# Moving PSUM evictions and one batch's normalisation from ScalarE to VectorE in a fused attention and gated-MLP kernel, with new instruction orders

## The chip, the core and the metric

The kernel runs on one core of a Trainium2 chip. Five engines work on their own instruction streams and meet only at semaphores: TensorE (PE in the profile, its weight loads PEld), VectorE (DVE), ScalarE (ACT), GpSimd (POOL) and SyncE (SP), which here issues every DMA. TensorE writes its results into PSUM; VectorE and ScalarE read them from there. The metric is the device time of one execution in microseconds (us). Three runs of the kernel before gave 223.18 us as the median, 222.97 the lowest and 224.26 the highest.

## What is computed

The inputs are q, k, v of 4 batches x 8 heads x 768 positions x 64 elements, and the weights of a gated MLP. Attention lets each query see only 6 chunks of 32 keys, chosen by an upper bound on the chunk's scores; the MLP mixes positions with a 768 x 768 matrix. Cut to what matters:

```python
ub = sum(max(q * k_min[chunk], q * k_max[chunk]))        # per query and chunk of 32 keys, causal
sel = the 6 chunks with the largest ub
attn = softmax(where(sel & causal, q @ k.T / 8, -1e9))
x = (attn @ v), heads side by side                       # 4 x 768 x 512
h = gelu_tanh(x @ w_in)                                  # 512 -> 1024
u, vg = h[..., :512], h[..., 512:]
v_n = (vg - mean(vg)) / sqrt(var(vg) + 1e-6) * g_ln
v_s = w_sg @ v_n + b_sg                                  # over the 768 positions
out = x + (u * v_s) @ w_out
```

## The kernel before

The unit of the attention is a pair of heads, 16 of them, numbered 0 to 15; four pairs make a batch, numbered 0 to 3 (the fourth to be done is batch 3). For each pair the kernel does the following; the names in brackets are the tags of the operations in the code, and they are used in all that follows.

- Rows of q and k are loaded by DMA (qn, kn), v too (vn). TensorE transposes them into PSUM (qtr, ktr, two halves each, line 508). The transposed q is copied out of PSUM (qev, line 561) and the transposed k too (kev, line 539; pairs 4 to 7 need two copies for each half, one for each head). VectorE reduces each chunk of k to its minimum and maximum (kmm, line 532). POOL makes a clipped q (rel, line 565), casts q (qcast, line 572), and casts v (vcast, line 577).
- The chunk bounds come from TensorE (ub, lines 602 and 649, for one pair or for two at once); VectorE transposes them (utr), finds the sixth largest (m8), compares (dn) and transposes back (dt). SP copies the resulting mask rows into place (qd) for pairs from 4 on.
- Scores (sc, lines 717, 757, 763) go to PSUM, ScalarE takes their exponential (exp, lines 723 and 772), POOL zeroes the part above the diagonal (aff, lines 728 and 779), TensorE multiplies by v (pv, and pvd for the diagonal blocks, which waits for aff; lines 795 and 802), VectorE divides by the row sum (rcp, xs; lines 810 and 812).

After the fourth pair of a batch its x is transposed (xtr, line 829; batch 2 by DMA) and copied out of PSUM as x^T (xev, line 832). Then the MLP of the batch runs, interleaved with the attention of later pairs: six products for the gate half (hv, line 844) with a GELU on ScalarE (gv, 848), mean and variance on VectorE (bns, bna, var), the inverse root on POOL (rstd, line 859, one instruction for the batch), the normalisation vhat (six instructions, line 874 on ScalarE or line 879 on VectorE), eight products for the other half (hu, line 890) with a GELU (gu, 895), eight products with w_sg (pt, line 907), a scale and a product on VectorE (vs, gt), six products with w_out (ou, line 926), the sum with x (os) and the store (st). The transposes of w_sg (wst) are copied out by VectorE (wev). The casts of w_in (wic) are POOL's, and hv of the first batch needs all four.

Two switches say which engine copies out of PSUM: a pair in KDVE or QDVE has its kev or qev on VectorE, otherwise on ScalarE; VH and XEV say for each batch which engine does vhat and xev. `evac` (line 423) emits the one instruction or the other. Where vhat is on ScalarE, POOL has two small instructions more (nmr, nmr2, lines 862 and 865). PSUM has two buffers for scores (PSC) and four for the rest (PSG); transposes mostly use two of these four, so a late eviction holds back the next transpose.

Nothing is ordered at run time. `_build` numbers the operations in the order in which it makes them; `TABLE` holds for each engine, SP's DMA queue included, the order in which it runs them, the PSUM buffer of each tile, and where TensorE gets extra idle matmuls that write nothing that is used (15 in all). `place` and `link` turn this into semaphore waits. An engine works strictly in its order, so an operation that waits holds everything behind it on its engine.

Of the kernel before, what the change touches and what calls it, by code (L numbers as in the profile page):

```python
# [260 lines left out]
def _build(nc, ctx, q, k, v, w_in, g_ln, w_sg, b_sg, w_out, out):  # L261
# [3 lines left out]
    F = DFF // 2  # L265
# [23 lines left out]
    def T(name, shape, dt):  # L289
        return ctx.enter_context(nc.sbuf_tensor(name, list(shape), dt))  # L290
# [25 lines left out]
    VH = ("act","dve","dve","dve")  # L316
# [10 lines left out]
    KDVE = (2,)  # L327
    QDVE = (2, 3)
    WEV = "dve"
    XEV = ("act",)*4  # L330
# [29 lines left out]
    vhat = [T(f"vhat{i}", [128, NT, F], BF16) for i in range(2)]  # L360
# [474 lines left out]
    def moe_h(b):  # L835
# [31 lines left out]
        for qt in range(NT):  # L867
# [5 lines left out]
            elif VH[b] == "act":  # L873
                P.op("act", lambda e, qt=qt: e.activation(vhat[s][:, qt, :], vg[qt], ACTF.Identity,  # L874
                                                          bias=nmr[s][:, qt:qt + 1], scale=rstd[s][:, qt:qt + 1]),
                     (F / 1.2 + 85, F / 1.2 + 185), ("vhat", b, qt),
# [107 lines left out]
    for p in range(4, NP + 4):  # L984
# [38 lines left out]
    "act": (  # L1023
# [11 lines left out]
    "dve": (  # L1035
# [34 lines left out]
        "2310011001113201111000110023011000001123101101222333233223233233322232222310110032101011032001101032"  # L1070
        "11000113200123010310311323203212101302"),
    "filler": (
        "43:9 54:1 59:3 77:2"),
}


# [57 lines left out]
```

## Time and profile before

| what | us |
|---|---|
| median of three runs | 223.18 |
| the profiled execution, its own time | 222.71 |
| its span, first to last instruction | 221.0 |
| TensorE busy | 204.0 |
| VectorE busy | 173.1 |
| ScalarE busy | 165.1 |
| GpSimd busy | 101.6 |

The profile is of one execution. Its page gives busy times, the chain of work that ended last, and groups of instructions; other views give the busy time of each engine in chosen stretches of the span, the instructions in order of time with the idle time ahead of them, and sums of waits by who waited for whom. In a row of a group, the number behind the bar is the busy time, then the mean length of one instruction in ns, then the idle time ahead of them. In a row of waits, the numbers are the sum in us, how often, and the longest.

### The profile page before, as it was taken

What the parts mean: (1) busy time and instruction counts of PE and PEld (TensorE: products, weight loads), DVE (VectorE), ACT (ScalarE), POOL (GpSimd) and SP (SyncE); (2) the same over time, 40 slices, a digit from 0 to 9 for tenths busy, and PEclk for the clock granted to TensorE, in tenths of its full rate; (3) what the DMA queues carried; (4) which work ended last, traced back from release to release, by engine and by line L of the source; (5) the groups of instructions that cost most, each with busy time, mean ns of one, the idle gap of its engine ahead of it and who ended that gap; (6) DMA issues with size and microseconds to landing.
All of it is one profiled execution on the core that took longest, in us unless ns stands there. A gap on an engine that the chain in (4) does not pass through costs nothing.

```text
span 221.0 us, 5927 instructions
## 1 busy us (share of the span) xinstructions
PE 204.0 (92%) x2332; PEld 133.8 (61%) x2348; DVE 173.1 (78%) x500; ACT 165.1 (75%) x249; POOL 101.6 (46%) x153
## 2 busy tenths in 40 slices
PE   7778999879979999988999999999799999999992
PEld 3356767745646667677556676777445669545641
DVE  3499684649949898885799998987698767688993
ACT  3857899987999696989868977899867898753000
POOL 6363975985416939745170057998402114001000
PEclk9999999999999999999999999999999999999998
DMA  7999999899077997895969977959502002001316
GB/s 152 220 241 237 230 227 334 180 243 310 14 201 202 214 205 216 197 200 127 200 135 215 188 185 164 266 133 154 155 6 77 20 0 98 0 3 74 116 55 230
DMA packets 87451, 35.47 MB, mean 160 GB/s; under 512 B 80129, under 2 KB 82433, under 8 KB 87425
## 3 DMA queue, kind: packets, MB, share of 16 engines
q1 hardware_dynamic: 87424, 35.11, 68.2%
q8 instruction: 18, 0.29, 0.6%
q14 instruction: 9, 0.07, 0.1%
HBM read 24.77 MB, written 6.29 MB: 141 GB/s over the span
## 4 chain that ended last, share of the span: by engine, by line
PE 60%; ACT 12%; DVE 10%; DMA 8%; POOL 4%; issue 2%; SPq 2%; DVEq 0%; POOLq 0%
PE PSG L907 14%; PE PSG L926 8%; PE PSC L717 7%; PE PSG L508 6%; PE PSG L844 6%; PE PSG L890 6%; DMA vn<-in_v_dram 6%; ACT E L772 4%; PE PSG L795 4%; PE PSG L649 3%; ACT vhat L874 2%; DVE W L532 2%; DMA qn<-in_q_dram 2%; ACT KA L425 2%; SPq L492 2%
## 5 line engine op out<-in xcount | busy, mean ns | idle before, releaser
L723 ACT ACTIVATE E<-PSC 128x1024 bf16<-128x1024 f32 (+1 forms) x72 | 63.4, 919 | 8.6 <-PE PSC L717 8.2
L532 DVE TENSOR_REDUCE W<-PSG 128x12 f32<-128x384 f32 x64 | 32.7, 544 | 9.8 <-PE PSG L508 9.6
L728 POOL TENSOR_SCALAR_AFFINE_SELECT E<-E 128x768 bf16<-128x768 bf16 x24 | 20.5, 863 | 41.2 <-ACT E L723 41.0
L717 PE MATMUL PSC<-QA,KA 128*128 128x128 bf16 (+2 forms) x336 | 37.2, 246 | 0.0
L907 PE MATMUL PSG<-wsgT,vhat 128*128 128x384 bf16 x192 | 35.0, 326 | 0.7 <-ACT vhat L874 0.5
L717 PEld LDWEIGHTS PSC<-QA,KA 128*128 128x128 bf16 x336 | 24.2, 98 | 8.6 <-ACT E L723 2.2
L895 ACT ACTIVATE uT<-PSG 128x384 bf16<-128x384 f32 x32 | 15.3, 489 | 16.0 <-PE PSG L890 15.7
L907 PEld LDWEIGHTS PSG<-wsgT,vhat 128*128 128x128 bf16 x192 | 17.9, 98 | 12.0 <-ACT vhat L874 0.8
L890 PE MATMUL PSG<-xT,winb 128*128 128x384 bf16 x128 | 24.1, 327 | 0.8 <-ACT uT L895 0.8
L572 POOL CAST QA<-qT 64x768 bf16<-64x768 f32 (+1 forms) x28 | 23.3, 836 | 2.8 <-ACT qT L425 1.6
L772 ACT ACTIVATE E<-PSC 128x1024 bf16<-128x1024 f32 (+1 forms) x24 | 20.8, 920 | 4.6 <-PE PSC L763 4.4
L913 DVE SCALAR_TENSOR_TENSOR PSG<-PSG,glnT,bsgbc 128x384 f32<-128x384 f32 x32 | 19.8, 621 | 5.6 <-PE PSG L907 5.2
L844 PE MATMUL PSG<-winb,xT 128*128 128x512 bf16 x91 | 21.6, 379 | 1.1 <-ACT qT L425 0.5
L926 PE MATMUL PSG<-woutb,uT 128*128 128x512 bf16 x86 | 21.6, 379 | 0.5
L795 PE MATMUL PSG<-vx,E 128*128 128x65 bf16 x480 | 19.9, 194 | 1.2 <-POOL vx L577 0.8
L425 ACT ACTIVATE KA<-PSG 128x384 bf16<-128x384 f32 (+1 forms) x38 | 18.4, 492 | 1.9 <-PE PSC L717 1.2
L795 PEld LDWEIGHTS PSG<-vx,E 128*128 128x128 bf16 x480 | 17.4, 98 | 3.6 <-POOL vx L577 1.1
L933 DVE TENSOR_TENSOR osb<-PSG,XS 128x512 f32<-128x512 f32 x24 | 16.2, 684 | 4.0 <-PE PSG L926 3.5
L853 DVE BATCH_NORM_STATS2 stats<-vgb 128x6 f32<-128x512 f32 x24 | 15.9, 684 | 4.0 <-ACT vgb L848 3.7
L917 DVE TENSOR_TENSOR uT<-PSG,uT 128x384 bf16<-128x384 f32 x32 | 17.6, 555 | 0.8
L848 ACT ACTIVATE vgb<-PSG 128x512 f32<-128x512 f32 x24 | 14.0, 597 | 5.4 <-PE PSG L844 4.6
L812 DVE TENSOR_TENSOR XS<-PSG,rden 128x384 bf16<-128x384 f32 x32 | 17.4, 552 | 0.7
(87 smaller groups left out, 337.1 us busy)
## 6 DMA issues: line engine op xcount, KB each, us to landing
kn<-in_k_dram SPq DMA_DIRECT2D x32, 192.0 KB, 4.5
qn<-in_q_dram SPq DMA_DIRECT2D x32, 192.0 KB, 4.4
vn<-in_v_dram SPq DMA_DIRECT2D x16, 384.0 KB, 5.1
out_dram<-osb SPq DMA_DIRECT2D x24, 256.0 KB, 2.4
uT<-in_moe_w_sg_dram SPq DMA_DIRECT2D x4, 384.0 KB, 5.0
KA<-INDF SPq DMA_DIRECT2D x16, 96.0 KB, 3.7
vgb<-in_moe_w_in_dram SPq DMA_DIRECT2D x3, 512.0 KB, 8.0
QA<-Dt SPq DMA_DIRECT2D x24, 36.0 KB, 2.4
```

Source lines behind the costliest of these rows:

```text
L425: P.op("act", lambda e: e.activation(dst(), src(), ACTF.Copy), act(n), tag, reads=reads, writes=writes, ps=ps, shift=shift)
L532: P.op("dve", lambda d, m=m, op=op, src=src, h0=h0, h1=h1: d.tensor_reduce(W[w][:, m, 12 * h0:12 * h1].rearrange("p (h c) -> p h c", h=h1 ...
L572: P.op("pool", lambda g, i=i, r0=r0, r1=r1: g.tensor_copy(QA[w][i or 0][r0:r1, :], qT[r][r0:r1, :]), gps(S, 250 if i == 1 else 150), ("qca ...
L717: r = e.matmul(t.ap()[:, o:o + n], KA[w][i][:, 128 * kb:128 * kb + 128], QA[w][i][:, q0:q0 + n], start=True, stop=True)
L723: P.op("act", lambda e, t=t, c0=c0, c1=c1, i=i: e.activation(E[es][:, i, c0:c1], t.ap()[:, 0:c1 - c0], ACTF.Exp, scale=SCALE), act(c1 - c0 ...
L728: P.op("pool", lambda g, ev=ev: g.affine_select(ev, ev, pattern=[[0, NT], [1, 128]], compare_op=ALU.is_ge, fill=0.0, base=0, channel_multi ...
L772: P.op("act", lambda e, t=t, c0=c0, c1=c1, n=n: e.activation(E[es][:, :, c0:c1], t.ap().rearrange("p (i x) -> p i x", i=2)[:, :, 0:n], ACT ...
L795: r = e.matmul(t.ap()[:, 65 * qb:65 * qb + 65], E[es][:, i, a:a + 128], vx[w][:, kb, i, :], start=first, stop=False, skip_group_check=True)
L844: r = e.matmul(t.ap()[:, 0:F], xT[s][:, dk, 128 * qt:128 * qt + 128], winb[:, dk, F:DFF], start=(dk == 0), stop=(dk == NDK - 1))
L890: r = e.matmul(t.ap()[:, 0:TG], winb[:, dk, 128 * fb:128 * fb + 128], xT[s][:, dk, TG * tg:TG * tg + TG], start=(dk == 0), stop=(dk == NDK ...
L907: r = e.matmul(t.ap()[:, 0:TG], vhat[s][:, sb, 128 * fb:128 * fb + 128], wsgT[:, sb, TG * tg:TG * tg + TG], start=(sb == 0), stop=(sb == N ...
L926: r = e.matmul(t.ap()[:, 0:DM], gT[s][:, fb, 128 * qt:128 * qt + 128], woutb[:, fb, :], start=(fb == 0), stop=(fb == NF - 1))
```

## The change

Four settings move work from ScalarE to VectorE, and every order in `TABLE` is replaced by another.

```diff
-    VH = ("act","dve","dve","dve")
+    VH = ("dve","dve","dve","dve")
...
-    KDVE = (2,)
-    QDVE = (2, 3)
+    KDVE = (2, 5)
+    QDVE = (2, 3, 4, 5)
     WEV = "dve"
-    XEV = ("act",)*4
+    XEV = ("dve","dve","act","dve")
...
-                     (F / 1.2 + 85, F / 1.2 + 185), ("vhat", b, qt),
+                     (705, 812), ("vhat", b, qt),
...
     "filler": (
-        "43:9 54:1 59:3 77:2"),
+        "54:9 43:1 81:2"),
```

In instructions: six vhat of batch 0, twelve xev of batches 0, 1 and 3 (batch 2 has none, it is transposed by DMA), four kev of pair 5 (two halves, two heads) and four qev of pairs 4 and 5 become VectorE's; nmr and nmr2 of batch 0 are gone from POOL. The cost pair of line 876 is read by nothing that runs. The extra idle matmuls go from 15 to 12.

The orders are lists of numbers (from 444 on, the same operation has a number two lower after the change). Read back into tags, these are the places of the new orders that the prediction speaks of; the old order stands first in each pair.

```
SP at the start    before: kn_0 kn_0 qn_0 qn_0 kn_2 qn_1 qn_1 kn_2 kn_1 kn_1 ...
                   after:  qn_0 qn_0 kn_0 kn_0 kn_1 kn_1 qn_1 qn_1 kn_2 kn_2 ...
VectorE, first     before: kmm_0 x4, utr_0 m8_0 dn_0, kmm_2 kev_2, dt_0, kmm_1 x4 ...
                   after:  kmm_0 x4, kmm_1 x4, utr_0 m8_0 dn_0 dt_0 ...
ScalarE, batch 0   before: ... exp_3_2 kev_5 kev_5 exp_3_3 qev_4 xev xev qev_4 xev qev_5 qev_5 gv_0_1 kev_5 kev_5 gv_0_0 ...
                   after:  ... exp_3_2 exp_3_5 gv_0_1 gv_0_0 gv_0_5 ...
VectorE, batch 0   after:  ... xs_2_1 qev_4 kev_5 kev_5 kmm_5 kmm_5 rcp_3_0 xev xs_3_0 rcp_3_1 xs_3_1 qev_5 xev qev_5 bns_0_1 ...
                           ... bna_0_4 dn_4 var_0 kmm_7 dt_4 kmm_7 vhat vhat wev_4 vhat vhat vhat wev_5 vhat kmm_6 kmm_6 vs_0_1_3 ...
POOL, batch 1      before: ... wsub_10 aff_8_1 vcast_8 qcast_10 rstd_1 aff_8_0 rel_13 vcast_9 wsub_13 rel_12 ...
                   after:  ... aff_8_1 wsub_10 wsub_11 rel_12 vcast_10 vcast_9 rstd_1 qcast_12 vcast_8 ...
POOL, pairs 11-13  before: ... aff_11_0 qcast_15 vcast_13 aff_12_0 vcast_15 vcast_14 wsub_14 aff_12_1 wsub_15 aff_13_1 ...
                   after:  ... aff_11_0 qcast_14 aff_11_1 qcast_14 qcast_13 rel_15 wsub_14 aff_12_0 qcast_15 aff_12_1 wsub_15 aff_13_1 ...
SP, v rows         before: ... vn_5 vn_4 ... qd_7_0 vn_7 st_0_0 qd_7_1 kn_10 qn_11 qn_11 vn_6 kcp_8 ...
                   after:  ... vn_4 ... st_0_2 vn_6 ... qd_6_1 st_0_1 qd_6_0 vn_5 ... st_0_5 kn_10 vn_7 ...
```

More of the change, by code (lines that the diff above doesn't have):

```diff
@@ L1006 @@
     "pe": (
[16 rows of a table removed]
-    "act": (
[11 rows of a table removed]
-    "dve": (
[16 rows of a table removed]
-    "pool": (
[14 rows of a table removed]
[16 rows of a table added]
+    "act": (
[9 rows of a table added]
+    "dve": (
[17 rows of a table added]
+    "pool": (
[14 rows of a table added]
     "slots": (
-        "1032203030210120010003201301110123012001010002312130100001102310101010110320101100333232223323232332"
-        "3223233223000110230110011010033101010101110032001001000112301111012332323233232222332323332232001101"
-        "2310011001113201111000110023011000001123101101222333233223233233322232222310110032101011032001101032"
-        "11000113200123010310311323203212101302"),
+        "0201213133101220001003102211100023010011000112331022110101102301000100101321110101333232323322232332"
+        "2223233323100111230000010010022111110101110032110101001103200111012332322233232322332223332332010101"
+        "2300000100102311111011100023011000011123011101222333233223233233322232223310110023101011032001101032"
+        "11000113202011300113121012230230013132"),
     "filler": (
-        "43:9 54:1 59:3 77:2"),
+        "54:9 43:1 81:2"),
 }
```

111 rows, old and new, of the table TABLE are left out of this document.

## The prediction, made before the changed kernel was run

> **What bounds the kernel now.** First the page's list of busy times (the span is 221.0), then the view that gives busy time by stretch, cut at the places where the work changes: the start, the attention of batch 0 (to the first hv), its MLP up to the first pt, then the rest.
>
> ```profile
> PE 204.0 (92%) x2332; PEld 133.8 (61%) x2348; DVE 173.1 (78%) x500; ACT 165.1 (75%) x249; POOL 101.6 (46%) x153
> ```
> ```profile
> core 0: us, PE busy (x) PEld busy (x) DVE busy (x) ACT busy (x) POOL busy (x), PEclk, DMA share, GB/s
> 0.00:13.40 13.40, 10.20 (x60) 5.20 (x61) 7.04 (x25) 7.09 (x12) 6.71 (x21) 1.00 1.09 191
> 13.40:46.60 33.20, 29.53 (x551) 21.95 (x553) 24.03 (x82) 28.93 (x42) 23.47 (x34) 1.00 1.03 243
> 46.60:65.10 18.50, 16.57 (x138) 9.53 (x140) 14.09 (x50) 16.41 (x31) 9.48 (x14) 1.00 0.68 181
> 65.10:95.40 30.30, 30.10 (x349) 21.09 (x353) 26.17 (x79) 25.09 (x38) 21.15 (x32) 1.00 0.92 209
> 95.40:107.20 11.80, 10.06 (x157) 8.02 (x155) 8.02 (x25) 10.81 (x16) 4.83 (x6) 1.00 0.76 156
> 107.20:145.00 37.80, 37.57 (x390) 25.14 (x395) 35.70 (x108) 30.41 (x48) 18.13 (x25) 1.00 0.88 195
> 145.00:158.40 13.40, 11.81 (x224) 9.34 (x224) 9.04 (x22) 12.18 (x18) 10.18 (x16) 1.00 0.73 144
> 158.40:190.00 31.60, 31.28 (x330) 19.86 (x331) 25.34 (x72) 25.92 (x36) 6.28 (x7) 1.00 0.13 44
> 190.00:221.00 31.00, 26.93 (x141) 13.62 (x142) 23.68 (x47) 8.28 (x15) 1.33 (x1) 0.98 0.23 85
> ```
>
> TensorE is the bound: 204.0 of 221.0. Its 17 us of idle time are all that any reordering can win, and they lie in few places. Length less busy time gives 3.20 us at the start, 3.67 in the attention of batch 0 (call it stage A), 1.93 in its MLP (stage B), 0.20 from 65.1 to 95.4, 1.74 up to 107.2 (stage C), 0.23 up to 145, 1.59 up to 158.4 (stage D), 0.32, and 4.07 at the end. The start waits for rows of q and k and the end for the last products and stores; the change touches neither in substance, since what stands first in the new orders still has to wait for the q and k of pair 0. So the question is what becomes of the 8.9 us in A to D. In A and B ScalarE is the busiest of the other engines, 28.93 of 33.20 and 16.41 of 18.50; in C 10.81 of 11.80.
>
> **The price of a moved instruction.** These are the groups by form: the four that leave ScalarE, and the nearest forms on VectorE. The single row behind them, from the instructions in order of time, shows six vhat on VectorE in one run.
>
> ```profile
> L874 ACT ACTIVATE vhat<-vgb,nmr,rstd 128x512 bf16<-128x512 f32 x6 | 4.6, 811 | 0.0
> ...
> L425 ACT ACTIVATE xT<-PSG 128x768 bf16<-128x768 bf16 x12 | 9.6, 809 | 1.6 <-PE PSG L829 1.6
> ...
> L425 ACT ACTIVATE KA<-PSG 64x384 bf16<-64x384 f32 x16 | 7.7, 483 | 0.4 <-DVE W L532 0.2
> ...
> L425 ACT ACTIVATE qT<-PSG 128x384 f32<-128x384 f32 x28 | 13.5, 489 | 4.4 <-PE PSG L508 3.8 <-POOL QA L572 0.4
> ...
> L428 DVE COPY wsgT<-PSG 128x768 bf16<-128x768 bf16 x6 | 3.3, 544 | 2.0 <-PE PSG L477 1.9
> ...
> L428 DVE COPY qT<-PSG 128x384 f32<-128x384 f32 x4 | 2.2, 550 | 0.2 <-PE PSG L508 0.2
> ...
> L879 DVE TENSOR_SCALAR vhat<-vgb,mv,rstd 128x512 bf16<-128x512 f32 x18 | 8.5, 542 | 0.9 <-POOL rstd L859 0.8
> ```
> ```profile
> 115.55 2.84 DVE L879 TENSOR_SCALAR vhat<-vgb,mv,rstd 128x512 bf16<-128x512 f32 x6
> ```
>
> ScalarE loses 4.6 for vhat, 9.6 for the twelve xev, 1.9 for four of the 16 half-height kev (7.7 / 4) and 1.9 for four of the 28 qev (13.5 / 7): 18.0 us, so 147 of 221 are left. On VectorE an instruction takes less of the queue than its length, because the next one begins before it ends: six vhat in 2.84 us is 0.47 each at a length of 542 ns, and so is 8.5 / 18. I take 0.47 for a vhat, and for the copies their rows less the same 0.07: 0.48 for a qev (row 550) and a kev, 0.48 to 0.54 and here 0.50 for an xev (the wsgT copy has its shape, type and source: 544). VectorE gains 6 x 0.47 + 12 x 0.50 + 8 x 0.48 = 12.7 us and stands at 185.8. An xev gets 0.27 us shorter in itself, a qev 0.06 longer.
>
> The Trainium skill, "VectorE: DVE Perf Modes", section "The DRAIN you can't avoid", says that the next VectorE instruction does not start until the pipe of the one before is empty. By that rule the 26 instructions would cost their full length, about 14.2 us, and VectorE's room in stage A, worked out below, would be 2.6 instead of 3.4 us. The row above speaks against it for instructions without a wait between them.
>
> **Stage A, 13.4 to 46.6.** Twelve of the moved instructions lie here or just behind: 4 kev, 4 qev, 4 xev. The end of the stage on ScalarE, in order of time:
>
> ```profile
> 38.38 0.81 ACT L425 ACTIVATE xT<-PSG 128x768 bf16<-128x768 bf16 x1
> ...
> 40.34 0.98 ACT L425 ACTIVATE KA<-PSG 64x384 bf16<-64x384 f32 x2
> ...
> 41.23 1.01 ACT L772 ACTIVATE E<-PSC 128x1024 bf16<-128x1024 f32 x1
> ...
> 46.01 0.87 ACT L425 ACTIVATE qT<-PSG 128x384 f32<-128x384 f32 x2
> ...
> 46.90 1.28 ACT L848 ACT_TABLE_LOAD   x1
> ```
> ```profile
> 44.77 0.50 PE L829 MATMUL PSG<-identB,XS 128*128 128x128 bf16 x6 [0.67 <-ACT qT L425]
> ...
> 46.78 0.81 PE L844 MATMUL PSG<-winb,xT 128*128 128x512 bf16 x3 [0.52 <-ACT qT L425]
> ```
>
> The row at 41.23 is the last exponential of pair 3, on which pv, xs, xtr, xev and so the first hv depend; ahead of it stand one xev and two kev that go, 0.81 + 0.98 = 1.8 us. Behind it TensorE waits twice for a qev (0.67 and 0.52), and the table for the GELU is loaded at 46.90 only because two qev stand ahead of it; with no copy between the last exponential and the first gv that load falls into ScalarE's idle time. That is the gain side. The other side is VectorE: 24.03 us busy and 12 x 0.48 to 0.50 = 5.8 more make 29.8 of 33.2, so the stage can shorten by at most 3.4 us, and only if VectorE never waits, where it now idles 9.2. Ends of the range: 0 and -3.4 (below nothing is the second rival). I take -1.5, near the 1.8 that leaves the queue in front of the last exponential, and less than that because VectorE has its share of idling. Rows of w_in are not behind this: the casts on POOL stand ahead of hv in both orders, and 23.47 of 33.20 leaves POOL room.
>
> **Stage B, 46.6 to 65.1.** The six vhat took ScalarE 4.6 us between gv, gu and two kev, and pt waits for the last of them. In the new order they follow rstd directly with two wev between: 6 x 0.47 + 2 x 0.50 = 3.8 us. ScalarE falls from 16.41 by 4.6, by 1.0 for two kev and by 1.3 for the load to 9.5; VectorE rises from 14.09 by 2.8, less one kmm (0.5) that goes behind vs, to 16.4. So VectorE allows 2.1, TensorE's idle time 1.93. Ends 0 and -1.9; I take -1.2. nmr and nmr2 on POOL are worth nothing, they ran beside rstd. Against it: ub_4 needs rel_5, which needs qev_5, now VectorE's very last instruction ahead of the MLP; the first hv covers 0.81 us of a copy and a rel (0.67, below). I add 0.3, between 0 and 0.6.
>
> **Stage C, 95.4 to 107.2.** Two waits of TensorE that the orders and the move touch:
>
> ```profile
> 96.93 0.63 PE L795 MATMUL PSG<-vx,E 128*128 128x65 bf16 x15 [0.80 <-POOL vx L577]
> ...
> 102.61 0.50 PE L829 MATMUL PSG<-identB,XS 128*128 128x128 bf16 x6 [0.33 <-ACT qT L425]
> ```
>
> The first is pv_6: the issue of v of pair 6 stands eleven places earlier on SP now. The other is ScalarE's queue, which loses four xev, 9.6 / 3 = 3.2 us. VectorE takes 2.0 and stands at 10.0 of 11.8: room for 1.8, TensorE's idle time 1.74. Ends 0 and -1.7; I take -1.0. On the other side v of pair 5 goes behind two qd_6 on SP, which wait for dt_6, and two os and a vs go ahead of dt_6 on VectorE:
>
> ```profile
> 79.64 0.78 DVE L677 STREAM_TRANSPOSE Dt<-Dn 128x576 bf16<-128x576 bf16 x1
> ...
> 80.34 0.65 DVE L933 TENSOR_TENSOR osb<-PSG,XS 128x512 f32<-128x512 f32 x1
> ```
> ```profile
> 90.34 0.62 PE L795 MATMUL PSG<-vx,E 128*128 128x65 bf16 x15
> ```
> ```profile
> vn<-in_v_dram SPq DMA_DIRECT2D x16, 384.0 KB, 5.1
> ```
>
> On the clock of before: dt_6 ends at 80.42 + 3 x 0.65 = 82.4, the issue some 2 later, 5.1 to land and 0.8 for the cast (1.61 for two, row below) make 90.3, and pv_5 began at 90.34. What is won ahead of it shifts both. I take 0; ends 0 and 1.3, two more instructions of that kind ahead of dt_6.
>
> **Stage D, 145 to 158.4.** Here nothing moves from ScalarE; the order of POOL changes.
>
> ```profile
> 150.23 0.35 PE L802 MATMUL PSG<-vx,E 128*128 128x65 bf16 x6 [0.50 <-POOL E L728]
> ...
> 153.41 1.61 POOL L577 CAST vx<-vn 128x768 bf16<-128x768 f32 x2 [0.88 <-DMA vn<-in_v_dram]
> ...
> 155.18 0.86 POOL L728 TENSOR_SCALAR_AFFINE_SELECT E<-E 128x768 bf16<-128x768 bf16 x1
> ...
> 156.10 0.54 PE L802 MATMUL PSG<-vx,E 128*128 128x65 bf16 x12 [1.09 <-POOL E L728]
> ```
>
> aff_12_1 (155.18) stood behind two casts of v that waited 0.88 us for their DMA; TensorE waited 1.09 for it, and 0.50 for aff_11_0. In the new order both casts come after aff_13_0. The 1.59 cannot all be had: ScalarE is busy 12.18 of 13.40, which leaves 1.2. I take -1.0, ends 0 and -1.2.
>
> **What else the new orders cost.** In batch 1 rstd now stands behind rel_12 and two vcast on POOL:
>
> ```profile
> L565 POOL TENSOR_SCALAR rT<-qT 128x576 f32<-128x576 f32 x16 | 10.7, 666 | 4.4 <-ACT qT L425 3.3 <-DVE qT L428 1.0
> ```
> ```profile
> 112.19 0.49 ACT L425 ACTIVATE qT<-PSG 128x384 f32<-128x384 f32 x1
> ...
> 114.07 1.34 POOL L859 TENSOR_TENSOR rstd<-rstd,neghalf 128x6 f32<-128x6 f32 x1
> ...
> 118.76 1.14 PE L907 MATMUL PSG<-wsgT,vhat 128*128 128x384 bf16 x6
> ```
>
> rel_12 needs the qev that ends at 112.68; 0.67 for it and 1.61 for two casts (the row at 153.41) give 115.0, where rstd began at 114.07. That is 0.9 later, and vhat ended at 115.55 + 2.84 = 118.4, 0.4 ahead of pt: +0.5 on the path, ends 0 and 1.4 (no slack). The long stretch to 145 has nothing to give (TensorE 37.57 of 37.80, VectorE 35.70); for order effects there and in the two other full stretches I add 0.2, from -0.3 to 1.0.
>
> **Sum.** -1.5 - 1.2 - 1.0 - 1.0 + 0.3 + 0.5 + 0.2 = -3.7. The profiled execution took 222.71 us, its span and 1.7 around it, so 219.0; the median of the runs is 0.47 above that execution, so 219.5 for a median.
>
> **The rivals.** *VectorE takes the place of ScalarE, no change.* If VectorE keeps 3.4 of its 9.2 us of idle time in A, 2.1 of 4.4 in B and 1.8 of 3.8 in C, the stages stay as long as they are; D gives 1.0, the new waits take 1.0, and the time is 223.2. For it: those idle times are waits for TensorE's results, which a fuller queue does not remove, and every transpose into the two shared PSUM buffers now waits for VectorE's turn. Against it: 29.8, 16.4 and 10.0 us still fit, and VectorE already runs at 35.70 of 37.80 elsewhere.
>
> *Slower: VectorE's idle time stays.* The same mechanism past its break-even, which is 37% of the idle time kept in A and 48% in B and C. With two thirds kept, A is 24.03 + 5.8 + 6.1 = 35.9 (+2.7), B 14.09 + 2.3 + 2.9 = 19.3 (+0.8), C 8.02 + 2.0 + 2.5 = 12.5 (+0.7); with D and the new waits cancelling that is 222.71 + 4.2, for a median 227.4.
>
> *All of it.* Each stage at its end, -3.4 - 1.9 - 1.7 - 1.2 = -8.2, and no new wait: 215.0.
>
> **How the numbers follow.** The forecast, gains of 2 to 5.5 us and so 217.7 to 221.5, gets 0.53; no change 0.22; slower 0.18; all of it 0.07. One per cent is 2.2 us, about what a measurement of this kernel can tell from no change. Faster takes the forecast without the 0.06 of it above 221, and the last case: 0.54. Same takes 0.22 + 0.06 = 0.28, slower 0.18. The range from 216.2 to 225.4 leaves out about 0.05 below and 0.15 above; the likeliest case's own is 217.7 to 221.5.
>
> **What would show it.** Right, if the first hv starts near 45.1 instead of 46.78, the table load ahead of it is done before hv ends, the first pt comes about 17.6 us after the first hv instead of 18.5, the 0.80 before pv_6 and the 1.09 before the diagonal blocks of pair 12 are gone, and VectorE is busy about 90% up to the first pt. Wrong, if TensorE's idle time in A and B is as long as before with VectorE named as what ended it, if rstd of batch 1 leaves a gap over 1.4 us ahead of pt, or if casts of v are waited for at pv_5.

## The result, and the profile after

The changed kernel takes 216.95 us (median of 4 runs, 215.63 to 218.14); the kernel before takes 223.59 (median of 4). The ratio is 0.970, 95% interval 0.963 to 0.977: 3% faster, where 3.7 us, 1.7%, was forecast. The profiled execution took 216.26 with a span of 214.5, 6.5 less than the 221.0 before. In the experiment with rstd first, two of the six executions, the profiled one (221.57) among them, were slow, so its time below is that of the other four, and its rows are read for what waits on what and not for how long.

Beside the orders, the new `TABLE` gives 110 of the 332 PSUM tiles another buffer. The runs below that keep the old orders keep the old buffers too, and those with the new orders have the new ones (experiment 8, which exchanges the lists of POOL and SP alone, has the new ones).

The busy times of the changed kernel, from its page:

```profile
PE 202.6 (94%) x2331; PEld 134.4 (63%) x2345; DVE 183.1 (85%) x526; ACT 149.9 (70%) x223; POOL 101.3 (47%) x151
```

VectorE gained 10.0 us with 26 instructions and ScalarE lost 15.2. TensorE's idle time fell from 17.0 to 11.9, which is 5.1 of the 6.5 us; the other 1.4 are busy time (204.0 before, 202.6 now), spread over many lines. The prediction had counted on idle time alone. The view by stretch, changed kernel, cut at the same events as the one of before (the columns are PE, PEld, DVE, ACT, POOL):

```profile
13.40:45.00 31.60, 29.19 (x554) 21.72 (x554) 28.57 (x94) 24.35 (x32) 24.55 (x36) 1.00 1.15 260
45.00:62.10 17.10, 16.41 (x141) 9.88 (x144) 15.29 (x52) 11.13 (x22) 8.55 (x11) 1.00 0.73 174
...
91.50:102.50 11.00, 10.91 (x167) 8.84 (x168) 10.07 (x35) 9.58 (x14) 8.41 (x11) 1.00 0.84 207
...
140.70:152.30 11.60, 11.52 (x221) 9.20 (x218) 9.22 (x22) 11.28 (x17) 9.02 (x13) 1.00 0.64 118
```

Length less the first number is TensorE's idle time: 2.41 in A (3.67 before), 0.69 in B (1.93), 0.09 in C (1.74), 0.08 in D (1.59). In B, C and D nearly all of it went. TensorE's rows of the changed kernel at the ends of the stages, in order of time:

```profile
40.68 0.63 PE L795 MATMUL PSG<-vx,E 128*128 128x65 bf16 x15 [0.70 <-ACT E L772]
...
43.78 0.51 PE L829 MATMUL PSG<-identB,XS 128*128 128x128 bf16 x6 [0.61 <-DVE XS L812]
...
45.17 0.81 PE L844 MATMUL PSG<-winb,xT 128*128 128x512 bf16 x3 [0.54 <-DVE xT L428]
46.16 0.72 PE L649 MATMUL PSG<-qT,W 64*32 64x288 f32 x16 [0.18 <-POOL rT L565]
...
62.24 1.14 PE L907 MATMUL PSG<-wsgT,vhat 128*128 128x384 bf16 x6
...
91.94 0.62 PE L795 MATMUL PSG<-vx,E 128*128 128x65 bf16 x15
...
93.02 0.62 PE L795 MATMUL PSG<-vx,E 128*128 128x65 bf16 x15
...
117.17 0.55 PE L508 MATMUL PSG<-identF,kn 128*128 128x128 f32 x3 [0.52 <-DMA kn<-in_k_dram]
...
150.20 0.35 PE L802 MATMUL PSG<-vx,E 128*128 128x65 bf16 x6
```

The first hv starts at 45.17, the first pt 17.07 later and without a wait. The products with v of pair 6 (91.94 and 93.02, one row for each head) and the diagonal products of pair 12 (150.20) have no bracket any more: those waits are gone. What is left in A is named by ScalarE once and by VectorE twice. ScalarE at the same place, changed kernel:

```profile
39.33 1.30 ACT L772 ACTIVATE E<-PSC 128x1024 bf16<-128x1024 f32 x2 [0.40 <-PE PSC L763]
40.65 1.28 ACT L848 ACT_TABLE_LOAD   x1
```

The table load follows the last exponential directly and has ended 3.2 us before the first hv.

The next table says where each kernel stands at five events, as starts of TensorE's work in us with the weight load included (so up to 0.23 ahead of the matmul's row). "Old" and "new" are the orders of before and of the changed kernel. The column for pair 6 is the start of the same products in all rows, those of its head 1: in the old orders they are the first of pair 6's two heads, in the new ones they follow head 0.

| kernel | first hv | first pt | pv of pair 6, head 1 | last hv, batch 1 | first hv, batch 2 | span |
|---|---|---|---|---|---|---|
| before | 46.55 | 65.12 | 96.92 | 109.93 | 158.38 | 221.0 |
| changed | 44.94 | 62.13 | 92.99 | 105.03 | 152.31 | 214.5 |
| moves in old orders | 48.50 | 69.53 | 102.56 | 115.39 | 163.60 | 226.2 |
| new orders, no moves | 47.56 | 67.67 | 99.04 | 113.36 | 160.34 | 222.7 |
| vhat back | 44.97 | 64.74 | 96.11 | 108.15 | 154.81 | 217.0 |
| copies back | 48.08 | 65.59 | 96.27 | 110.60 | 157.83 | 220.2 |
| POOL's order in D only | 46.87 | 65.45 | 97.39 | 110.39 | 157.82 | 220.4 |
| v of pair 6 early | 46.98 | 65.55 | 97.63 | 110.84 | 158.85 | 221.5 |
| old POOL and SP orders | 55.86 | 73.08 | 108.63 | 120.60 | 176.16 | 238.4 |
| four copies doubled | 47.15 | 64.77 | 96.37 | 108.42 | 155.55 | 217.8 |
| four copies back | 44.53 | 61.68 | 93.68 | 106.02 | 152.85 | 215.1 |

From row two less row one: A gives 1.61, B 1.38, the stretch to pair 6 0.94, C's rest 0.97, from there to batch 2 1.17, the end 0.43. Each row is one execution, and a few tenths are scatter: kernels with the same orders up to the first hv have it at 46.55, 46.87 and 46.98 (before, POOL's order in D only, v of pair 6 early) and at 44.94, 44.87 and 44.39 (changed, and experiments 6 and 9). Most of that lies ahead of the first scores, which start at 13.49 before and at 13.96 in the changed kernel. From the first scores to the first hv it is 33.06 before and 30.98 in the changed kernel, 2.1 less.

### The profile page after: what moved, and what is told of

Its sections match the earlier page's. It is cut to its first block, busy times and chain, and to the rows that moved or that the text cites. A ratio compares the mean times of both kernels' runs of the same rounds, so it can differ in the third digit from the quotient of the medians.

```text
span 214.5 us, 5915 instructions
## 1 busy us (share of the span) xinstructions
PE 202.6 (94%) x2331; PEld 134.4 (63%) x2345; DVE 183.1 (85%) x526; ACT 149.9 (70%) x223; POOL 101.3 (47%) x151
## 4 chain that ended last, share of the span: by engine, by line
PE 72%; DVE 11%; ACT 7%; DMA 4%; issue 2%; SPq 1%; POOL 1%; DVEq 0%
PE PSG L907 13%; PE PSC L717 12%; PE PSG L926 9%; PE PSG L844 7%; PE PSG L508 7%; PE PSG L795 6%; PE PSG L890 5%; DVE W L532 3%; ACT E L772 3%; PE PSG L649 3%; PE PSG L802 2%; DMA kn<-in_k_dram 2%; PE PSC L367 2%; PE PSG L829 2%; PE PSC L757 2%; ACT KA L425 2%
## 5 line engine op out<-in xcount | busy, mean ns | idle before, releaser
L848 ACT ACTIVATE vgb<-PSG 128x512 f32<-128x512 f32 x24 | 14.2, 597 | 13.9 <-PE PSG L844 13.0
L565 POOL TENSOR_SCALAR rT<-qT 128x576 f32<-128x576 f32 x16 | 10.9, 683 | 15.7 <-ACT qT L425 11.0
```

## The experiments

The two theories at the outset: the gain comes from relieving ScalarE (theory 1), or from the orders, whichever engine copies (theory 2).

### 1. The moves alone, in the old orders

```diff
 (settings VH, KDVE, QDVE, XEV as in the changed kernel; all orders as before, but:)
-ScalarE:  ... each xev, kev_5, qev_4, qev_5 of the 20 at its place
+VectorE:  ... the same instructions, at the time at which ScalarE had run them
-ScalarE:  vhat_0 x6 between gv, gu and kev
+VectorE:  ... dn_4 dt_4 wev_3 vhat_0 x6 kmm_7 kmm_7 wev_4 ...
```

> The old orders with all 26 instructions moved to VectorE, each put into VectorE's old order at the time it had on ScalarE (the six vhat behind wev_3); nothing else is reordered. Theory 1, relieving ScalarE is what wins in batch 0 and ahead of batch 1: 220 to 221.5, the first hv 1 to 2 us earlier, the first pt 2 to 3 us earlier, the wait of 1.09 ahead of the diagonal blocks of pair 12 still there. Theory 2, the new orders win and the engine of a copy matters little: 223 to 224, or 1 to 3 us slower because VectorE's order was not made for it.

227.21 us (226.76 to 227.94), ratio 1.018 (1.011 to 1.024): slower than before. The two waits of TensorE just ahead of the first hv, its longest one of B, VectorE ahead of that, and the view of B, all of this kernel:

```profile
46.41 0.51 PE L829 MATMUL PSG<-identB,XS 128*128 128x128 bf16 x6 [1.34 <-DVE qT L428]
...
48.73 0.81 PE L844 MATMUL PSG<-winb,xT 128*128 128x512 bf16 x3 [0.82 <-DVE qT L428]
...
67.32 0.49 PE L477 MATMUL PSG<-identB,wsb 128*128 128x128 bf16 x6 [2.84 <-DVE wsgT L428]
```
```profile
62.46 3.31 DVE L879 TENSOR_SCALAR vhat<-vgb,mv,rstd 128x512 bf16<-128x512 f32 x6
65.70 1.01 DVE L532 TENSOR_REDUCE W<-PSG 128x12 f32<-128x384 f32 x2
66.63 0.54 DVE L428 COPY wsgT<-PSG 128x768 bf16<-128x768 bf16 x1
```
```profile
48.50:69.50 21.00, 16.93 (x137) 10.32 (x140) 19.20 (x58) 11.23 (x22) 9.15 (x12) 0.97 0.68 177
```

The two waits before hv that ScalarE's qev had caused (0.67 and 0.52) are now VectorE's, and longer. Six vhat in one run and two kmm stand in front of a wsgT copy that frees the buffer of the next transpose, and TensorE stops for 2.84. VectorE had room by its busy time (19.20 of 21.00); the copies stood at the wrong places. The granted clock of the stage is 0.97: from 68.05 to 71.47, right behind the long wait, it is 0.50. TensorE is busy for 206.5 us in this kernel and for 204.0 before, so a part of the 4.4 us lost is slower work and not waiting. Theory 1 falls.

### 2. The new orders without the moves

```diff
 (orders as changed, but the 26 moved instructions on ScalarE again, each at the time at which VectorE had run it; nmr, nmr2 on POOL again; settings as before)
```

> The new orders with all 26 instructions back on ScalarE, each at the time it had on VectorE; POOL has nmr and nmr2 of batch 0 again. Theory 1: 219.5 to 221.5, the first hv and the first pt about where they were before, pair 12 without its wait. Theory 2: 216.5 to 218.

224.47 us (224.07 to 225.93), ratio 1.007 (1.004 to 1.011). TensorE in this kernel:

```profile
43.43 0.63 PE L795 MATMUL PSG<-vx,E 128*128 128x65 bf16 x15 [1.68 <-ACT E L772]
...
66.83 0.88 PE L508 MATMUL PSG<-identF,kn 128*128 128x128 f32 x6 [1.68 <-ACT KA L425]
```

Theory 2 falls too. Against before (223.59 and 222.85 in the two sessions), the moves alone cost 4.4 and the orders alone 1.6, and both together gain 6.6. Theory 3, formed here: every eviction needs a place in a strict queue, and moves and orders only win as a pair. What the two runs do not show is that the copies have to be on VectorE: they stand at times taken from the other engine's order, and no run looked for the best places on ScalarE for all 26 (experiment 11 does it for four).

### 3 and 4. One half of the moves back

```diff
 vhat back:   the six vhat of batch 0 on ScalarE at VectorE's times, nmr and nmr2 on POOL; the rest as changed
 copies back: xev, kev_5, qev_4, qev_5 on ScalarE at VectorE's times; vhat stays on VectorE
```

> The new kernel with only the six vhat of batch 0 back on ScalarE. Theory 1: the first pt about 1.4 us later after the first hv, 218 to 219, and nothing else changes. Theory 2: 216.5 to 217.5.

> The new kernel with the twelve xev, four kev and four qev back on ScalarE, vhat left on VectorE. Theory 1: the first hv about 1.5 us later, stage C about 1 us longer, 219 to 220. Theory 2: 216.5 to 217.5.

Vhat back: 219.00 us (218.73 to 222.01), ratio 0.984 (0.975 to 0.993). Copies back: 222.05 us (221.51 to 222.96), ratio 0.995 (0.992 to 0.999). By the medians the vhat are worth 2.0 us and the copies 5.1, together 7.1, where taking both back costs 7.5: within the new orders the two halves add up, as far as intervals of one to two us can tell. By the table the vhat work in B alone (the first hv is where it was, the first pt 2.61 later); the copies cost 3.14 up to the first hv and 2.29 between pair 6 and the last hv of batch 1. The kernel with vhat back, TensorE and ScalarE:

```profile
63.90 0.88 PE L508 MATMUL PSG<-identF,kn 128*128 128x128 f32 x6 [1.68 <-ACT KA L425]
```
```profile
62.17 0.48 ACT L895 ACTIVATE uT<-PSG 128x384 bf16<-128x384 f32 x1
62.54 0.81 ACT L874 ACTIVATE vhat<-vgb,nmr,rstd 128x512 bf16<-128x512 f32 x1
63.36 0.48 ACT L425 ACTIVATE KA<-PSG 64x384 bf16<-64x384 f32 x1
```

A copy of k of pair 7 (63.36) stands behind a vhat and a GELU, with one more vhat ahead of these, and the transpose of k of pair 6, which needs the buffer that it frees, waits 1.68. The kernel with the copies back, ScalarE around the last exponentials of pair 3:

```profile
39.49 0.82 ACT L425 ACTIVATE xT<-PSG 128x768 bf16<-128x768 bf16 x1
40.18 1.04 ACT L772 ACTIVATE E<-PSC 128x1024 bf16<-128x1024 f32 x1
...
42.00 0.48 ACT L425 ACTIVATE KA<-PSG 64x384 bf16<-64x384 f32 x1 [0.41 <-DVE W L532]
42.39 0.36 ACT L772 ACTIVATE E<-PSC 128x256 bf16<-128x256 f32 x1
```

The last exponential starts at 42.39; in the changed kernel both are done at 40.63. A copy ahead of it has itself to wait for a kmm (0.41). This is the step of stage A as forecast. It is not all of the 3.14 us, as the view of this kernel up to its first hv shows:

```profile
13.40:48.10 34.70, 30.65 (x552) 22.76 (x552) 23.45 (x82) 29.00 (x42) 24.60 (x36) 0.95 1.11 256
```

TensorE is busy for 30.65 us, where the changed kernel has 29.19 for as much work: from 43.03 to 46.45 its granted clock is 0.50. So 1.5 of the 3.1 us are slower work, and the waits gave the other half. The slow stretch begins right behind TensorE's wait of 1.68 for the last exponential, which ended at 42.81. The kernel without the moves has a wait of the same length (43.43, experiment 2) and its profiled execution no such stretch there, so when a wait has this price stays open.

### 5. POOL's order in stage D alone

```diff
 (before, POOL only)
-... aff_10_0 qcast_15 rel_15 qcast_14 aff_11_0 ... vcast_15 vcast_14 wsub_14 aff_12_1 wsub_15 aff_13_1 ...
+... aff_10_0 aff_11_0 qcast_15 rel_15 qcast_14 ... wsub_14 aff_12_1 wsub_15 aff_13_1 vcast_15 vcast_14 ...
```

> The kernel before, with POOL's order changed at one place only: the two casts of v of pairs 15 and 14 go behind the last diagonal mask of pair 13, and the first diagonal mask of pair 11 moves up right behind the one of pair 10. No instruction leaves ScalarE. Theory 1 (stage D is bound by the masks' place on POOL, and nothing else of the change is needed there): the waits of 0.50 and 1.09 us ahead of the diagonal products of pairs 11 and 12 are gone, from the scores of pair 12 to the second hv of batch 2 it takes about 9.4 us instead of 11.0, everything ahead of it stays, and the time is 1.0 to 1.6 us less, a ratio near 0.994. Rival (ScalarE is the limit of stage D, or the casts of v behind the masks make a wait of their own): the waits move to another engine and the time is within 0.3 us of before.

222.03 us (220.41 to 222.72) against 223.06 for the kernel before in the same session, ratio 0.995 (0.992 to 0.998). The same stretch, from the last products with w_out of batch 1 to the first hv of batch 2 (the expectation's "second hv"), in this kernel, in the one before and in the changed one:

```profile
145.80:157.80 12.00, 11.60 (x221) 9.16 (x220) 8.63 (x21) 11.42 (x17) 8.30 (x12) 1.00 0.63 143
```
```profile
145.30:158.40 13.10, 11.51 (x222) 9.13 (x221) 8.74 (x21) 11.88 (x18) 10.01 (x15) 1.00 0.72 140
```
```profile
141.00:152.30 11.30, 11.22 (x219) 9.07 (x217) 8.92 (x21) 10.98 (x16) 8.72 (x13) 1.00 0.65 118
```

POOL's places alone give 1.1 of the 1.8 that this stretch became shorter, with both waits gone, and theory 1's number for D holds. The rest goes with the new orders of the other engines: TensorE has 0.4 less to do in the stretch and 0.3 less idle time, and ScalarE, at 97% of it, has 16 instructions there, against 18 before.

### 6. rstd of batch 1 first

```diff
 (changed, POOL only)
-... wsub_10 wsub_11 rel_12 vcast_10 vcast_9 rstd_1 ...
+... wsub_10 wsub_11 rstd_1 rel_12 vcast_10 vcast_9 ...
```

> The changed kernel, with one step of POOL's order put back: rstd of batch 1 goes ahead of the relative-position add of pair 12 and of the casts of v of pairs 10 and 9. Theory (my step for it, +0.5 us, was a real cost): rstd starts about 1 to 2 us earlier, the idle time of TensorE ahead of the first pt of batch 1 goes, and the time is 0.4 to 0.8 us less. Rival: the late rstd lies beside other work of TensorE, or the two casts of v and the rel behind it become late for pair 9, 10 and 12 instead, and the time is the same within 0.3 us or longer.

218.4 us (217.71 to 218.91), ratio 0.978 (0.974 to 0.983): not faster than the changed kernel; the median is 1.5 us above it, with intervals that overlap. The theory falls: that step was no cost to be had back. This kernel's POOL, VectorE, SP and TensorE:

```profile
110.40 1.34 POOL L859 TENSOR_TENSOR rstd<-rstd,neghalf 128x6 f32<-128x6 f32 x1 [1.97 <-DVE rstd L857]
...
112.35 1.80 POOL L577 CAST vx<-vn 128x768 bf16<-128x768 f32 x2
```
```profile
112.89 3.37 DVE L879 TENSOR_SCALAR vhat<-vgb,mv,rstd 128x512 bf16<-128x512 f32 x6
```
```profile
113.21 0.37 SPq L500 DMA_DIRECT2D vn<-in_v_dram  x1
```
```profile
116.40 2.11 PE L907 MATMUL PSG<-wsgT,vhat 128*128 128x384 bf16 x12 [0.39 <-DVE vhat L879]
120.84 0.55 PE L508 MATMUL PSG<-identF,kn 128*128 128x128 f32 x3 [2.33 <-DMA kn<-in_k_dram]
```

Two things happen. The vhat start at 112.89, 1.15 after rstd's end, because VectorE's own list has transposes and maxima first (at 112.23 it still runs maxima for 0.74); rstd did not hold them. And the casts of v, now behind rstd, free their buffer later: the issue of v of pair 13 waits at the head of SP's list until 113.21, with k of pair 12 four places behind it, and TensorE waits for that k, 2.33 us in this execution. In the changed kernel the cast comes first, SP goes on at 109.34, and rstd ends just in time:

```profile
108.60 0.74 DVE L857 TENSOR_SCALAR rstd<-mv 128x6 f32<-128x6 f32 x1
...
111.58 2.81 DVE L879 TENSOR_SCALAR vhat<-vgb,mv,rstd 128x512 bf16<-128x512 f32 x6
```
```profile
108.48 1.61 POOL L577 CAST vx<-vn 128x768 bf16<-128x768 f32 x2
110.06 1.34 POOL L859 TENSOR_TENSOR rstd<-rstd,neghalf 128x6 f32<-128x6 f32 x1
```

### 7. v of pair 6 early

```diff
 (before, SP only)
-... st_0_2 st_0_1 qd_6 qd_7 vn_7 st_0_0 qd_7 kn_10 qn_11 qn_11 vn_6 ...
+... st_0_2 vn_6 st_0_1 qd_6 qd_7 vn_7 st_0_0 qd_7 kn_10 qn_11 qn_11 ...
```

> The kernel before, with one transfer issued earlier: v of pair 6 goes nine places forward on SP, right behind the store of t of pair 0 of that stage's list, so that the 0.80 us that TensorE waited in front of the products with v of pair 6 should go. Theory 1 (that wait was on the path): the products of pair 6 start 0.8 us earlier and the time is 0.4 to 0.8 us less. Rival (ScalarE's queue sets the end of stage C, so the wait only moves to the transposes behind it): the products start earlier, the first hv of batch 1 does not, and the time is the same within 0.3 us.

222.66 us (221.21 to 223.18) against 223.06, ratio 0.997 (0.994 to 1.000). The wait of 0.80 ahead of pair 6 is gone, and the profiled execution has another of 1.13 earlier:

```profile
89.07 0.61 PE L795 MATMUL PSG<-vx,E 128*128 128x65 bf16 x15 [1.13 <-ACT E L723]
```

The edit made this wait itself. In the kernel's order these products need the PSUM buffer that VectorE frees with a sum with x (os_0_4), and that sum needs its output tile back from the store st_0_1, which the edit put behind v of pair 6 on SP. This kernel's VectorE:

```profile
88.23 0.69 DVE L933 TENSOR_TENSOR osb<-PSG,XS 128x512 f32<-128x512 f32 x1 [1.75 <-DMA out_dram<-osb]
```

The sum waits 1.75 us for the store and ends at 88.92, 0.15 ahead of the products. So the run does not tell what the early v is worth by itself. At most 0.6% came of it, perhaps nothing: undecided.

### 8. The old orders of POOL and SP

```diff
 (changed; POOL and SP in the orders of before)
```

> The changed kernel with the orders of POOL and SP of the kernel before; the orders of TensorE, VectorE and ScalarE and the moved instructions stay as changed. Theory 3 (the placing of the copies on TensorE, VectorE and ScalarE is what moves and orders win together; POOL and SP matter in stages C and D alone): the first hv and the first pt come within 0.5 us of the changed kernel's, the 0.8 us ahead of pair 6 and the 1.6 us of stage D are lost again, and the time is 2 to 3 us longer, near 219.5. Rival (the orders of all engines must fit each other from the start): waits on POOL and on loads show up in the first 60 us, the first pt is 2 us or more later, and the time is at 222 or above.

240.11 us (239.35 to 240.69), ratio 1.075 (1.070 to 1.080). My expectation of 219.5 was wrong by 20 us, and the rival is right. Sums of TensorE's waits in this kernel (us in all, times, longest):

```profile
PE PSG L795 <- POOL vx L577: 3.6, 2, 2.1
PE PSG L802 <- POOL E L728: 2.0, 1, 2.0
PE PSG L602 <- POOL W L551: 2.0, 1, 2.0
PE PSC L717 <- DMA KA<-INDF: 1.5, 1, 1.5
```

The first hv is already 10.9 us late. POOL is nowhere near full (101 us of 238), and yet the two old orders, under new ones for the other engines, cost more than everything else tried here; which of the two costs how much was not separated. TensorE is busy for 209.6 us here and for 202.6 in the changed kernel, at a granted clock of 0.979 and 0.999 in the mean, so up to 7 of the 23 us are slower work behind the waits.

### 9 to 12. Is the changed kernel at its end?

```diff
 kn_12 early (changed, SP):    - ... kn_12 qn_14 ... vn_13 kcp_10 qd_8 kn_13 kn_12 ...
                               + ... kn_12 kn_12 qn_14 ... vn_13 kcp_10 qd_8 kn_13 ...
 four copies doubled (changed, in evac, VectorE's branch, pair 5's kev only):
+    e.tensor_copy(an idle tile, src())
     e.tensor_copy(dst(), src())
 four copies back (changed, kev_5 on ScalarE):
-... exp_3 exp_3 exp_3 exp_3_5 gv_0_1 ...
+... kev_5 kev_5 exp_3 exp_3 exp_3 exp_3_5 kev_5 kev_5 gv_0_1 ...
 both: four copies back and kn_12 early
```

> The changed kernel, with one transfer issued earlier: the second half of k of pair 12 goes nine places forward on SP, right behind the first half, ahead of v of pair 13, whose issue waits until its buffer is cast. Theory (in the changed kernel TensorE waits 0.52 us in front of the first transpose of k of pair 12 because this load stands behind v of pair 13, and with rstd put first 2.33 us for the same reason): that wait is gone and the time is 0.3 to 0.6 us less than the changed kernel's 216.95, a ratio to the kernel before near 0.968. Rival (the transposes of pair 12 have slack behind them, or the load pushes others back): the wait goes and shows up within the next 20 us somewhere else, and the time is the same within 0.3 us.

216.37 us (215.94 to 216.60), ratio 0.971 (0.969 to 0.974). The wait of 0.52 is gone and nothing takes its place: from the last hv of batch 1 to the last products with w_out this kernel takes 35.35 us, the changed one 35.95, the one before 35.38. The medians differ by 0.58, as the theory has it, but the intervals overlap, so the time does not decide.

> The changed kernel with extra work: each of the four copies of k of pair 5 that now stand on VectorE is done twice, the second time into an idle tile, 4 times about 0.48 us more on VectorE in stage A; the output is that of the reference. Theory (VectorE has room in stage A because its queue keeps waiting for TensorE anyway; it was busy 27.8 of 30.7 us there): the first hv is 0.2 to 0.9 us later and the time 0 to 1 us longer than the changed kernel's. Rival, from my prediction (VectorE's idle time cannot be used, the queue is what sets the stage): the first hv is 1.5 to 1.9 us later and the time is 1.5 to 2 us longer, about 218.8.

219.39 us (218.74 to 220.03), ratio 0.985 (0.982 to 0.988): 2.4 us more for 1.9 us of work. TensorE in this kernel (its lines are six higher here), where the changed kernel has no wait at these three places:

```profile
38.37 0.63 PE L801 MATMUL PSG<-vx,E 128*128 128x65 bf16 x15 [0.24 <-DVE KA L434]
39.54 0.55 PE L514 MATMUL PSG<-identF,qn 128*128 128x128 f32 x3 [0.35 <-DVE wsgT L434]
...
44.83 0.55 PE L514 MATMUL PSG<-identF,qn 128*128 128x128 f32 x3 [1.02 <-DVE xT L434]
```

VectorE was idle for 3.0 us of stage A in the changed kernel, and none of it took the extra copies at these places: the first hv is 2.21 later, of which 0.41 was there at the first scores already, so 1.8 of 1.9. The rival holds.

> The changed kernel, with the four copies of k of pair 5 back on ScalarE, at two places of its queue where it idled: two ahead of the second exponential of pair 3 and two behind the last but one. Theory 3 (the place in the queue decides, and ScalarE has such places again once the other eight copies of stage A have left it): the first hv comes within 0.5 us of the changed kernel's and the time is within 1 us of 216.95. Rival (every copy on ScalarE in stage A delays the exponentials, the engine decides): the first products of pair 3 are about 1 us later, the first hv 1 us or more later, and the time is 218 or above.

215.70 us (215.23 to 217.13), ratio 0.969 (0.966 to 0.972), the lowest median of all, and not distinguishable from the changed kernel's. The first hv is 0.41 earlier, 0.33 of which it has from the start of the kernel. So taking four copies off VectorE wins nothing that can be told from the noise, though putting four more on costs all of their time. Theory 3 holds here: ScalarE has places for them, and for these four copies the engine does not matter. This kernel's ScalarE:

```profile
38.99 1.30 ACT L772 ACTIVATE E<-PSC 128x1024 bf16<-128x1024 f32 x2 [0.39 <-PE PSC L763]
40.60 0.98 ACT L425 ACTIVATE KA<-PSG 64x384 bf16<-64x384 f32 x2 [0.31 <-DVE W L532]
41.60 1.28 ACT L848 ACT_TABLE_LOAD   x1
```

Two of the copies stand behind the last exponential (not the last but one, as the expectation has it) and ahead of the table load, where ScalarE has nothing else to do.

> The changed kernel with both edits tried alone before: the four copies of k of pair 5 back on ScalarE at its idle places, and the second half of k of pair 12 issued right behind the first. Theory (VectorE and ScalarE fill stage A about equally, so moving four copies between them wins nothing there, and the wait of 0.52 us in front of pair 12 is on the path): first hv, first pt and stages C and D as in the changed kernel, no wait ahead of pair 12, and a time of 215.2 to 216.5, a ratio to the kernel before near 0.968. Rival (each of the two gives its own gain and they add): 214.5 to 215.2, a ratio of 0.965 or less.

216.07 us (215.59 to 217.32), ratio 0.971 (0.968 to 0.975). No gain of two edits that add up is seen. With the three variants at 215.7 to 216.4 beside 216.95 and overlapping intervals, none is shown to be better than the changed kernel; all beat the kernel before.

## Why the prediction was right or wrong

The direction, the places and most of the mechanism were right; the size was forecast at 3.7 us of span and was 6.5. The gain of 6.6 in the median lies outside the likeliest case's own 2 to 5.5, between it and "all of it". By the steps of its sum, with the measured terms from the table:

- **Stage A**, forecast -1.5: measured -1.6 at the first hv, and -2.1 counted from the first scores, which came 0.5 later in this execution. The first hv at 45.17 (45.1 forecast), the table load out of the way, VectorE at 90% (28.57 of 31.60). The copies-back run shows the cause that was named, copies ahead of the last exponential, and that about half of what they cost there is TensorE's slower clock behind its wait, for which the prediction had no term. VectorE kept 3.0 of its 9.2 us of idle time, a third; the break-even was put at 37%, and the doubled copies show that they could not use this third where they stood.
- **Stage B**, forecast -1.2 and +0.3: measured -1.4 (-0.8 and -1.2 in experiments 6 and 9, which have the same orders up to there). The relief was taken too small, since TensorE's idle time went from 1.93 to 0.69, and the wait of ub_4 was 0.18 instead of 0.3. The vhat-back run confirms that the vhat are the cause; the moves-alone run, where they stand in one run ahead of a wev, has the wait of 2.84.
- **Stage C**, forecast -1.0: measured -1.9 from the first pt to the last hv of batch 1, with 1.65 of the stage's 1.74 us of TensorE's idle time gone. This is the largest miss. "VectorE takes 2.0 and stands at 10.0 of 11.8: room for 1.8" was right (10.07 of 11.00), and I took 1.0 of the 1.7 that it allowed. The only reason that the prediction has for taking less, VectorE's share of idling in A, did not apply here: VectorE kept 0.9 of 3.8. Between the two parts only the copies are shown (2.3 in the copies-back run, after pair 6); the early v alone gave nothing sure, and made a new wait. v of pair 5 behind the qd cost nothing, as forecast.
- **Stage D**, forecast -1.0: measured -1.7 from the last products with w_out of batch 1 to the first hv of batch 2. POOL's part was right (1.0 in the median, 1.1 in the stretch). "ScalarE is busy 12.18 of 13.40, which leaves 1.2" was the failed bound: what an engine has to do in a stretch is not fixed when its order changes, and two instructions left it.
- **rstd of batch 1**, forecast +0.5, and other order effects +0.2: from the last hv of batch 1 to the last products with w_out it became 0.57 longer, close to the forecast by luck, for the reason is another: it is the wait of 0.52 for k of pair 12, which the early k takes away, and the prediction had no step for that load. The late rstd leaves no wait in front of pt, and putting it first gives nothing, because the casts that it goes ahead of free a buffer that SP's list waits for.
- **The end**, forecast 0: -0.4, not looked into.
- **VectorE's price**, 12.7 us for 26 instructions: right. Between before and changed VectorE's busy time grew by 10.0 only, but that difference mixes two things. In the old orders the moves raise it from 173.1 to 185.7, by 12.6. The new orders alone lower it, from 173.1 to 171.6, and with them the moves add 11.5: more instructions there follow each other without a gap and overlap, and busy time counts the overlap once. The rule that the prediction quotes from the Trainium skill, "VectorE: DVE Perf Modes", section "The DRAIN you can't avoid", gave 14.2, which no run here shows; the same section adds that an instruction that is not held starts earlier. ScalarE's relief, put at 18.0, was 15.2 (15.5 in the old orders).

The rivals: "no change" and "slower" both rested on VectorE's idle time staying. It is a real mechanism, and it is what the moves-alone run shows at 227.21, by chance next to the 227.4 that the second was priced at, for a part of it is the slower clock: with the old orders VectorE was idle for 6.5 of 35.1 us in A. The new orders are what kept it away, and the prediction, which read the copies and the orders as separate terms, had no term for that.

## What to carry to other kernels

Where every engine works in a fixed order, the move of an instruction and its place cannot be priced apart: here the moves alone cost 4.4 us, the orders alone 1.6, and both together gain 6.6. Idle time of the engine that takes the work is no room by itself; ask of each moved instruction what waits behind it and whether the thing it frees is needed next. A queue that is half empty still counts: POOL's and SP's old orders, under new ones elsewhere, cost 23 us, and a late cast on POOL held back a load of something else through SP's list. A load moved forward on a list does the same to what it overtakes: v of pair 6 held back a store, the store a sum on VectorE, and the sum TensorE.

## What the runs showed that I had not expected

TensorE's clock can halve behind a wait. In four of the profiles one or two stretches of 3.41 or 6.83 us at a granted clock of 0.50 lie inside the kernel: behind the wait of 2.84 of the moves-alone kernel, of 1.68 with the copies back, of 2.33 with rstd first, and twice with POOL's and SP's old orders (behind 1.96 and 2.02). Before and in the changed kernel there is none from the first scores to the last microseconds. Where one lies, the wait's price is more than the wait: 1.5 us more in stage A of the copies-back kernel.

VectorE and POOL hold each other up at times. The small instruction of line 857 took 0.74 us in the changed kernel beside two casts of v on POOL (the rows of both stand under experiment 6): it ended at 109.34, when the first of the two casts, which began at 108.48, was just over. Over the 14 profiles it ran 56 times: 0.73 to 0.75 the eight times that it began about 0.12 behind the start of such a cast, 0.48 or 0.49 the five times that it began about 0.36 behind the start of a cast of q, each time ending with the cast, and 0.16 or 0.17 all other times. The six vhat took 2.81 in the changed kernel with POOL idle, and 3.37 beside the two casts when rstd came first, which in turn became 1.80 long instead of 1.61; in the moves-alone kernel it was 3.31 beside a single cast of w_sg (0.89 instead of 0.82). The Trainium skill, "SBUF — State Buffer", section "Who interferes with whom", says that certain VectorE instructions share a pair of ports with GpSimd, and that the one that issues first has it for its whole length. The 0.74 and the 0.48 that end with the cast agree; whether line 857's instruction is of the kind that the page means, no run shows. Half a microsecond at a time, this is also a price that a moved instruction brings along, and none of my steps had it.
